# Subtractions of s2 one by one, sums of w_in in x's buffers, and one turning of x two places later

## The chip, the cores and the metric

The kernel runs on one core of one Trainium2 chip. The metric is the device time of one execution in microseconds (us), lower is better. A profile, taken in a separate execution, gives the start and the length of every instruction on each engine: TensorE (PE, with its weight loads as PEld), VectorE (DVE), ScalarE (ACT), GpSimd (POOL), and SyncE (SP), which here only starts transfers.

## What is computed

The first half is an attention without softmax: for each batch and head `kv = k^T v` and `out = q kv`, then each row of 64 is divided by its root mean square and multiplied by `g_norm`. The second half is a feed-forward block in fp32 on the 4608 x 512 result x:

```
h = x @ w_in                     # 4608x512 @ 512x2048
g = s * relu(h)**2 + b
out = g @ w_out                  # 4608x2048 @ 2048x512
```

## The kernel before, in words

**Units.** The 4608 rows are worked through in nine units of 512 rows, `u = 0..8`. Each unit has a first stage (x times w_in, with relu and square) and a second stage (g times w_out). While unit u is multiplied, the attention of unit u+1 is done in small pieces between the products; the dictionaries returned by `sides` and `side_of` say at which place of the order each piece goes, and `at(n)` runs what is filed under n.

**Seven products instead of eight.** A block product of 2 x 2 blocks is done with the seven products of the Strassen-Winograd scheme. They are numbered 1 to 7 and are always issued in an order like 1, 2, 6, 7, 5, 3, 4. They need sums of blocks of each operand: with a for one operand, `s1 = a21 + a22`, `s2 = s1 - a11`, `s3 = a11 - a21`, `s4 = a12 - s2`. From unit 2 on the scheme is used at two levels: in the second stage each of the seven products (its weights called 1 to 7) is itself split into seven small products; the pairs (2, 5) and (7, 3) go through together. In the first stage, products 2 and 3 are split (`small`).

**Names.** In `mm1_deep(u)`, the first stage of units 2 to 8, `run` writes the order out by hand. `x1, x6, x5, x3` are products into a PSUM tile called x_ps, `y7, y4` into one called y_ps; the number in brackets is the block s = 0..3 of 512 hidden columns. Within a tile a later product adds to an earlier one: `y4(3)` adds to what `y7(3)` wrote, after VectorE's `a22(3)` has read the first state. `small(i, pair, m, ...)` issues small products m into sx_ps and z_ps, each followed on VectorE by an addition that takes the state out (`r` or a part of `a`). `s1(s)` and `s3(s)` are the additions and subtractions above on g, one instruction of 128 x 512 each.

In `mm2(u)` the function `rest` is the second stage of units 2 to 8. `do_25(6)` issues product 6 of the pair (2, 5) and then VectorE's instruction that takes it out; `go_25(7)` issues the product alone. The take-out instructions are called `r1`, `r2`, `r4` (kept in the tile r) or go straight to the output tile o; all have line L1090. Products 1, 6, 5, 3 of a group add up in the same x_ps tile, so 5 may not be written until `r2` has read the state after 6, and 3 not until `r4` has read the state after 5. `sums_25((3,))` makes the operand sums for product 3 of the pair; `s2(...)` overwrites the blocks `a11` by `s1 - a11`, `s4(...)` the blocks `a12`, both one instruction of 128 x 512 for each of four blocks; `x3_s3` is the last such subtraction of the first stage.

**Order.** There is no scheduler: each engine executes its instructions in the order in which the program issues them, and waits on semaphores for what it needs from others. PSUM tiles x and y have two buffers each, z has one.

**Sums of the weights.** The sums of w_out's blocks for the lower level are made once, in the second stage of unit 1 (`parts_of_w`, called after every second product): four VectorE instructions write four tiles named `sub`, and GpSimd starts four transfers that put them into DRAM. `sums_of_w_in(key)` does the same for three blocks of w_in (`DEEP`): four VectorE instructions of 128 x 256 into two `sub` tiles, two transfers. In unit 1 all of these take tiles from one pool with tag "sub" and six buffers; a buffer can be written again when the transfer that reads it is done. In units 2 to 8 the operand sums of the second stage use the same six buffers, and those for product 7 two more with tag "sub7". The tiles `xs_4` to `xs_7` hold the sums of x for the first stage; between the last product of one unit's first stage and `x_sums(u + 1)` late in its second stage they are free.

**Weights.** The second stage's weights come through a ring of 14 buffers (`w_sb`), refilled by transfers from SyncE's queue as products finish (`used`, `pump`).

The order of `rest` around the change, before:

```
do_25(2); at(1); do_25(6)
step["x3_s3"](); s2(); sums_25((3,))
go_25(7); sums_6((5, 6)); do_25(5)
sums_6((7,)); do_6(1); s4((0, 1)); at(2); sums_6((3,)); do_25(3)
```

## Time and profile before

| | |
|---|---|
| time, median of 3 runs | 943.86 us (943.70 to 944.11) |
| span of the profiled execution | 940.1 us |
| TensorE busy | 909.8 us, 97% |
| VectorE busy | 695.0 us, 74% |
| ScalarE busy | 255.9 us, 27% |
| GpSimd busy (starting transfers) | 223.5 us, 24% |
| mean granted TensorE clock | 0.995 |

TensorE is the engine that is nearly always busy, so the time is the sum of its products plus the time in which it has nothing to do. Its products are the same before and after any change of order, so the places to look at are the gaps between them, what ended each gap, and what the engine named there had been doing. Busy shares of the other engines are means over stages in which their load differs much, and say little about a single gap.

### The profile page before, as it was taken

What the parts mean: (1) busy time and instruction counts of PE and PEld (TensorE: products, weight loads), DVE (VectorE), ACT (ScalarE), POOL (GpSimd) and SP (SyncE); (2) the same over time, 40 slices, a digit from 0 to 9 for tenths busy, and PEclk for the clock granted to TensorE, in tenths of its full rate; (3) what the DMA queues carried; (4) which work ended last, traced back from release to release, by engine and by line L of the source; (5) the groups of instructions that cost most, each with busy time, mean ns of one, the idle gap of its engine ahead of it and who ended that gap; (6) DMA issues with size and microseconds to landing.
All of it is one profiled execution on the core that took longest, in us unless ns stands there. A gap on an engine that the chain in (4) does not pass through costs nothing.

```text
span 940.1 us, 19143 instructions
## 1 busy us (share of the span) xinstructions
PE 909.8 (97%) x7524; PEld 831.8 (88%) x7524; DVE 695.0 (74%) x1259; ACT 255.9 (27%) x463; POOL 223.5 (24%) x418
## 2 busy tenths in 40 slices
PE   7999999999999899999999999999999999999998
PEld 6788888887989898899888988999899988999998
DVE  2789777787659867787678766886687777874685
ACT  2773132201225014500342033401450035002500
POOL 2000027024630323702281027303520300020000
PEclk9999999999999999999999999999999999999999
DMA  9688948159944884379436844585547812891275
GB/s 261 225 287 253 251 116 241 41 177 339 313 113 124 263 270 145 79 248 307 148 82 209 290 155 141 158 272 197 162 117 242 276 34 58 257 301 46 61 234 177
DMA packets 120137, 180.33 MB, mean 192 GB/s; under 512 B 29168, under 2 KB 46320, under 8 KB 120048
## 3 DMA queue, kind: packets, MB, share of 16 engines
q1 hardware_dynamic: 101552, 153.00, 52.3%
q0 software_dynamic: 15040, 23.88, 8.7%
q10 hardware_dynamic: 3456, 2.23, 0.9%
q8 instruction: 60, 0.98, 0.4%
q14 instruction: 29, 0.24, 0.1%
HBM read 153.36 MB, written 25.69 MB: 190 GB/s over the span
## 4 chain that ended last, share of the span: by engine, by line
PE 83%; DVE 8%; DMA 3%; issue 2%; ACT 2%; POOL 1%; ACTq 0%; DVEq 0%; POOLq 0%
PE x_ps L91 43%; PE y_ps L91 25%; PE z_ps L91 8%; PE sx_ps L91 4%; DVE a L253 2%; PE kv_ps L382 2%; PE y_ps L561 2%; DMA w<-sub 2%; DVE sub L253 2%; DMA kv_sb<-in_v_dram 1%; ACT a L806 1%; DVE xT L605 1%; DVE r L1090 1%; ACT a L805 1%; POOL w L1105 1%
## 5 line engine op out<-in xcount | busy, mean ns | idle before, releaser
L1616 POOL DMA_DIRECT2D q_sb<-in_q_dram x256 | 143.7, 570 | 138.2 <-issue 100.7
L91 PE MATMUL x_ps<-w_sb,sub 128*128 128x128 f32 x1176 | 152.7, 279 | 15.5 <-DVE r L1090 15.5
L91 PEld LDWEIGHTS x_ps<-w_sb,sub 128*128 128x128 f32 x1176 | 142.1, 195 | 17.7 <-DVE r L1090 17.0
L1202 POOL DMA_DIRECT2D out_dram<-o x110 | 54.8, 505 | 421.8 <-DVE o L1090 301.0
L91 PE MATMUL y_ps<-xs,wb 128*128 128x256 f32 x512 | 121.4, 382 | 0.0
L91 PE MATMUL x_ps<-xs,ws 128*128 128x256 f32 x512 | 121.3, 380 | 0.0
L91 PEld LDWEIGHTS y_ps<-xs,wb 128*128 128x128 f32 x512 | 94.4, 190 | 14.5 <-issue 2.3
L91 PEld LDWEIGHTS x_ps<-xs,ws 128*128 128x128 f32 x512 | 93.9, 190 | 11.4 <-issue 0.4
L826 ACT COPY a<-x_ps 128x512 f32<-128x512 f32 x28 | 16.4, 586 | 270.1 <-PE x_ps L91 270.1
L91 PE MATMUL x_ps<-xT,wa 128*128 128x256 f32 x384 | 89.1, 381 | 0.1
L250 DVE TENSOR_TENSOR r<-sx_ps,a 128x256 f32<-128x256 f32 x63 | 26.4, 420 | 74.0 <-PE sx_ps L91 73.9
L91 PEld LDWEIGHTS x_ps<-xT,wa 128*128 128x128 f32 x384 | 71.2, 190 | 11.1 <-issue 1.3
L91 PE MATMUL x_ps<-w_sb,a 128*128 128x128 f32 (+1 forms) x432 | 65.1, 299 | 1.8 <-DVE or L1090 1.8
L91 PE MATMUL y_ps<-w_sb,a 128*128 128x128 f32 (+1 forms) x416 | 63.9, 301 | 0.0
L91 PEld LDWEIGHTS x_ps<-w_sb,a 128*128 128x128 f32 x432 | 58.9, 191 | 5.4 <-DVE or L1090 2.2
L1090 DVE SCALAR_TENSOR_TENSOR r<-x_ps,s_col,o 128x256 f32<-128x256 f32 (+1 forms) x84 | 34.8, 414 | 34.0 <-PE x_ps L91 33.1
L91 PEld LDWEIGHTS y_ps<-w_sb,a 128*128 128x128 f32 x416 | 57.9, 197 | 2.1
L91 PE MATMUL y_ps<-w_sb,sub 128*128 128x128 f32 x392 | 49.5, 275 | 0.0
L253 DVE TENSOR_TENSOR a<-a,a 128x512 f32<-128x512 f32 x72 | 46.8, 684 | 1.2 <-ACT a L805 0.5
L250 DVE TENSOR_TENSOR a<-y_ps,r 128x512 f32<-128x512 f32 x36 | 24.8, 688 | 30.0 <-PE y_ps L91 22.3
L91 PE MATMUL z_ps<-w_sb,a 128*128 128x128 f32 (+1 forms) x352 | 46.8, 280 | 0.0
L91 PEld LDWEIGHTS y_ps<-w_sb,sub 128*128 128x128 f32 x392 | 46.6, 192 | 0.0
(190 smaller groups left out, 1488.4 us busy)
## 6 DMA issues: line engine op xcount, KB each, us to landing
w_sb<-w SPq DMA_DIRECT2D x385, 256.0 KB, 4.3
w<-sub POOLq DMA_DIRECT2D x34, 256.0 KB, 6.5
w_raw<-in_moe_w_in_dram SPq DMA_DIRECT2D x8, 1024.0 KB, 7.6
w_raw<-in_moe_w_out_dram SPq DMA_DIRECT2D x8, 1024.0 KB, 5.1
w_sb<-w SPq DMA_DIRECT2D x14, 512.0 KB, 8.1
w_sb<-in_k_dram SPq DMA_DIRECT2D x24, 288.0 KB, 4.8
w_sb<-in_v_dram SPq DMA_DIRECT2D x24, 288.0 KB, 4.9
out_dram<-o POOLq DMA_DIRECT2D x92, 64.0 KB, 3.3
```

The lines of the kernel that those rows point to most:

```text
L91: nc.tensor.matmul(o, lhsT=lhsT, rhs=rhs, start=start, stop=stop, skip_group_check=True)
L250: nc.vector.tensor_tensor(out=o, in0=a, in1=b, op=ALU.add)
L253: nc.vector.tensor_tensor(out=o, in0=a, in1=b, op=ALU.subtract)
L382: nc.tensor.matmul(ps[r][(r ^ l) * HB : (r ^ l) * HB + HB, i, :], lhsT=kv[l][0][rows, j, :], rhs=kv[l][1][rows, j, :], start=(j == 0), sto ...
L561: nc.tensor.matmul(ps[l][32 * p : 32 * p + 32, r, lo:hi], lhsT=bd_kv[b % 2][rows, p, at : at + 32], rhs=st["qT"][rows, p, lo:hi], start=Tr ...
L605: nc.vector.transpose(out=xT[u][:, :, j * P : j * P + 2 * P], in_=st["xn"].rearrange("p (c x) -> p c x", c=KC),)
L805: nc.scalar.activation(t, t, AF.Relu)
L806: nc.scalar.square(t, t)
L826: nc.scalar.copy(g_tile("a11", s), st["x", s])
L1090: nc.vector.scalar_tensor_tensor(o, ps, s_col, other, ALU.mult, ALU.add)
L1202: queues[s % 2].dma_start(out=view[b, jj, :, cols], in_=st[name, j][s * w : s * w + w, cols])
L1616: load()
```

## The change

Four things are changed, none of which alters a product or its order on TensorE:

1. In `rest`, the subtraction `x3_s3` and the first of four `s2` subtractions come before the taking out of product 6 of the pair (2, 5), and the other three are put one by one between the readings of the pair's products. The sums for group 6 and group (7, 3), and `s4`, are put later.
2. In `run`, `s1(1)`, `s3(0)`, `s3(1)` and the side work `at(17)` come after the small products 5, 3 and 4 of (2, 1). At 17 units 3 to 7 have the turning of x for the next unit (`turn_x`, a 128 x 1024 transpose), unit 2 has `back`, and unit 8 nothing.
3. `sums_of_w_in` takes buffers of the sums of x (`xs_5` and `xs_6`, then `xs_7` and `xs_4`, then `xs_5` and `xs_6` again) in place of two `sub` buffers, and its second and third call come at places 6 and 8 of unit 1's second stage in place of 7 and 9.
4. `parts_of_w` takes one of its four tiles from the two buffers "sub7", so that three, not four, come from "sub".

It is meant to shorten VectorE's unbroken blocks of work between readings of PSUM, and to keep the sums of the weights from waiting for buffers.

```diff
-    def sums_of_w_in(key):
+    def sums_of_w_in(key, tags):
...
         t = [
-            late["sub"].tile([P, FC // 4, P], FP32, name="sub", tag="sub", bufs=6) for _ in range(2)
+            xp.tile([P, KH, TB], FP32, name=f"xs_{n}", tag=f"xs_{n}").rearrange(
+                "p k (b n) -> p (k b) n", n=P
+            )
+            for n in tags
         ]
...
             a22(2)
             y7(3)
             s1(0)
-            s1(1)
-            at(17)
             small(2, 1, 5)
             x3(2)
+            small(2, 1, 3, 4)
+            s1(1)
             s3(0)
             s3(1)
-            small(2, 1, 3, 4)
+            at(17)
             early()
             at(18)
             y4(2)
...
             t1, t2, t3, t4 = (
-                late["sub"].tile([P, FC // 4, P], FP32, name="sub", tag="sub", bufs=6) for _ in range(4)
+                late["sub"].tile(
+                    [P, FC // 4, P], FP32, name="sub", tag="sub7" if m == 7 else "sub",
+                    bufs=2 if m == 7 else 6,
+                )
+                for m in (5, 6, 7, 4)
             )
...
             do_25(2)
             at(1)
+            step["x3_s3"]()
+            s2((0,))
             do_25(6)
-            step["x3_s3"]()
-            s2()
+            s2((1,))
             sums_25((3,))
             go_25(7)
+            s2((2,))
+            do_25(5)
+            s2((3,))
+            sums_6(())
+            do_6(1)
             sums_6((5, 6))
-            do_25(5)
-            sums_6((7,))
-            do_6(1)
-            s4((0, 1))
             at(2)
-            sums_6((3,))
             do_25(3)
-            sums_73((5, 6), 7)
+            sums_6((7, 3))
             do_25(4)
...
             do_6(2, 6)
+            s4((0, 1))
             s4((2, 3))
             go_6(7)
             do_6(5)
+            sums_73((5, 6), 7)
             sums_73((5, 6), 3)
             go_73(1)
...
+        of_w_in = [
+            partial(sums_of_w_in, *with_tags)
+            for with_tags in zip(DEEP, ((5, 6), (7, 4), (5, 6)))
+        ]
...
-            6: [B["norm"]],
-            8: [B["turn_x"], B["scale"]],
+            6: [B["norm"], of_w_in[1]],
+            8: [B["turn_x"], B["scale"], of_w_in[2]],
             11: [sums],
             13: [partial(loads, 3, 1)],
-            **{n: [partial(sums_of_w_in, key)] for n, key in zip((3, 7, 9), DEEP)},
+            3: [of_w_in[0]],
```

## Prediction
> **What bounds the kernel now.** I read the page's table of engines first: TensorE is the bound.

> ```profile
> PE 909.8 (97%) x7524; PEld 831.8 (88%) x7524; DVE 695.0 (74%) x1259; ACT 255.9 (27%) x463; POOL 223.5 (24%) x418
> ```

> No product changes, so only TensorE's gaps can move the time. The view of waits, for TensorE alone (total us, times, longest), lists them; what is left out has to do with the start of the kernel.

> ```profile
> PE x_ps L91 <- DVE r L1090: 15.5, 8, 2.1
> PE sx_ps L91 <- DVE r L250: 2.8, 6, 0.5
> PE x_ps L91 <- DVE or L1090: 1.8, 1, 1.8
> ```

> I then went through TensorE's timeline for where these are. The first row is one gap of 2.1 in each of units 2 to 8 (7 x 2.12) and one of 0.72 in unit 2; the second is one gap in each of units 2 to 7; the third is in unit 1. The timeline of unit 4 shows the first two (start, length, what; in square brackets the gap ahead):

> ```profile
> 486.12 1.89 PE L91 MATMUL x_ps<-xT,ws 128*128 128x256 f32 x8
> 488.46 0.71 PE L91 MATMUL sx_ps<-xT,w_sb 128*128 128x128 f32 x4 [0.45 <-DVE r L250]
> ...
> 495.59 1.89 PE L91 MATMUL y_ps<-xs,wb 128*128 128x256 f32 x8
> ...
> 509.82 1.95 PE L91 MATMUL x_ps<-w_sb,sub 128*128 128x128 f32 x16
> 511.61 1.06 PE L91 MATMUL x_ps<-w_sb,a 128*128 128x128 f32 x8
> 514.78 2.05 PE L91 MATMUL x_ps<-w_sb,sub 128*128 128x128 f32 x16 [2.12 <-DVE r L1090]
> ```

> And VectorE's timeline beside them shows why: product 5 of the pair is ready at 511.8, but its reading r4 (514.25) stands behind a block of s2 subtractions and sums.

> ```profile
> 508.24 0.49 DVE L1090 SCALAR_TENSOR_TENSOR r<-x_ps,s_col,o 128x256 f32<-128x256 f32 x1 [1.30 <-PE x_ps L91]
> 508.64 0.68 DVE L253 TENSOR_TENSOR a<-a,a 128x512 f32<-128x512 f32 x1
> 509.24 2.49 DVE L253 TENSOR_TENSOR a<-s,a 128x512 f32<-128x512 f32 x4
> 511.65 0.69 DVE L253 TENSOR_TENSOR sub<-a,sub 128x512 f32<-128x512 f32 x1
> ...
> 514.25 0.48 DVE L1090 SCALAR_TENSOR_TENSOR r<-x_ps,s_col,o 128x256 f32<-128x256 f32 x1
> ```

> Unit 1's gap (TensorE resumes at 230.77) has another cause: VectorE waits for `sub` buffers that transfers still read, with the reading of x_ps (230.27) queued behind.

> ```profile
> 227.35 0.69 DVE L253 TENSOR_TENSOR sub<-w_sb 128x512 f32<-128x512 f32 x1 [1.31 <-DMA w<-sub]
> 228.50 0.69 DVE L253 TENSOR_TENSOR sub<-w_sb,sub 128x512 f32<-128x512 f32 x1 [0.45 <-DMA w<-sub]
> 229.11 1.24 DVE L605 STREAM_TRANSPOSE xT<-xn 128x1024 f32<-128x1024 f32 x1
> 230.27 0.44 DVE L1090 SCALAR_TENSOR_TENSOR or<-x_ps,s_col,b_row 128x256 f32<-128x256 f32 x1
> ```

> Last, windows of 1 us show the granted clock (before the DMA share) after the 2.1 us gaps. In units 3, 6 and 8 it is about 0.5 for some 3.2 us, in the others 1.00:

> ```profile
> 416.00:417.00 1.00, 1.00 (x7) 1.00 (x6) 1.00 (x3) 0.00 (x0) 0.00 (x0) 0.50 0.63 215
> 516.00:517.00 1.00, 1.00 (x11) 1.00 (x10) 1.00 (x3) 0.00 (x0) 0.00 (x0) 1.00 0.09 31
> ```

> [...]between 210 and 250 us the windows have a DMA share of 0.92 to 1.01, so waits for transfers there are waits for bandwidth.

> **Prices from unit 4.** VectorE, start to start: 0.60 for a 128x512 sum, 0.72 if the next one needs its result, 0.40 for a 128x256 take-out (0.51 if needed), 0.26 for a 128x128 one, 0.34 for an addition in the first stage (0.45), 1.16 for the 128x1024 transpose. TensorE: 0.89 for 8 and 1.79 for 16 products of 128, 1.73 for 8 of 256, 0.45 for 4 of 128. From the end of a product to its reader 0.20 (506.25 + 1.79 to 508.24), from the end of a reading to the next product 0.05 (514.25 + 0.48 to 514.78). Laying out the old order with these gives 2.22 for the large gap and 0.63 for the small one, in start times; the busy rows show 0.1 to 0.2 less because a product's modelled end is late.

> **1. rest, on the path.** Product 6 of the pair ends at 508.04. Ahead of it VectorE idles 1.30 us, and x3_s3 and s2(0) now fit there (506.85 to 508.05). Then r2 508.24, s2(1) 508.64, two sums to 510.45, s2(2) to 511.05, idle until product 5 is done (509.82 + 1.79 + 0.20 = 511.81), r4 511.81 to 512.29. Product 3 could start at 511.61 + 0.89 = 512.50 and does: the gap of 2.2 goes. What was put later comes back once: after r2 of group 6 (518.06) stand four s4 (2.4), then r4 at 520.7, harmless, as product 73(1) ends only at 521.43; then the output of 5, four sums (2.6), two small outputs, and r1 of (7, 3) starts at about 524.75, so that product 73(6) starts at 525.25 and not at 525.0, a new gap of 0.24. Net gain 1.96 a unit; in unit 2, whose `norm` also lies there, the gap of 0.72 shrinks as well while two of 0.2 appear, net 2.1.

> **2. run, on the path, and against the change.** The small gap goes: r for small product 5 starts at 486.33 in place of 488.02, so small product 3 follows x3(2) at 487.85 in place of 488.46. Gain 0.61. But now the readings of small products 3 and 4 are queued ahead of s1(1), s3(0), s3(1) and turn_x, and VectorE has nothing to do from 487.09 until product 3 is read at 488.50 (487.85 + 0.45 + 0.20). It had no such idle time before. After product 4 (488.94 to 489.28) come s1(1), two s3, turn_x, two early sums, the four operations of y4(2), s1(2), s3(2): 0.6 + 1.2 + 1.16 + 1.2 + 2.72 = 6.9 us, so a22(3) reads y_ps at 496.1 to 496.8 in place of 494.57. TensorE wants y4(3), which overwrites that state, at 487.85 + 2 x 0.45 + 2 x 1.73 + 0.89 + 1.73 = 494.82, and gets it at 496.85. New gap 2.03; net loss 1.40 to 1.42. In unit 2 `back` takes the place of turn_x with 1.23, and ScalarE's square of it holds up the copy of x5(3): the same 2.1, part of it ahead of x3(3). Unit 8 has nothing at 17: the gap is 2.03 - 1.16 = 0.87, and it had no small gap to win, so it loses 0.97.

> **3. Sums of w_in and sub7, unit 1.** A buffer "sub" is now reused two calls of parts_of_w later (13.8 us) in place of six tiles (some 7 to 10 us). Transfers take 6.5 us in the median, 8.2 at most from their start. So the waits of VectorE (7.7 us in eleven waits) go. The call for weight 5 starts at 222.96, takes 2.5, turn_x 1.16, the sums of w_in now ahead of the reading 1.5; r4 at about 228.15, done at 228.65, just before x3(0) ends at 228.76. The gap of 1.84 goes. New is that `x_sums` for unit 2 waits until the last sums of w_in have left xs_5 (written by 228.2, transfer started about 229, landed by 237 to 238). VectorE may stand 4 to 5 us there; queued behind are two outputs, the last parts_of_w and x's sums for unit 2. The first product that needs xs_6 starts at about 243.6, and the work from 238 takes until 240.4 for xs and 245.6 for the first r, wanted at 247.05. So I cost it at nothing: y4(0), y4(1) and x1 of unit 2 hide it.

> Sum: units 3 to 7 win 1.96 - 1.40 = 0.56 each, 2.8; unit 2 2.1 - 1.4 = 0.7; unit 8 1.96 - 0.97 = 1.0; unit 1 1.8. Together 6.3. Clock: three half-clock windows of 3.2 us cost 1.6 each before; six gaps of 2.0 at 3 in 7 make 2.6 after, 0.6 us less, which I leave out. 943.86 - 6.3 = 937.5.

> **Rivals.**
> A: the gap before y4(3) does not appear (VectorE's order matters less than I think). Then each unit wins 2.6 (units 3 to 7), 2.8 and 1.9, with unit 1 19.4: 924.5. For it: two of VectorE's operations ahead of a22(3) would have to overlap more than the old order shows. Against: in the old order a22(3) starts only 1.02 before y4(3), so there is little slack.
> B: only the clock differs. All seven gaps give half clock: four more than now at 1.6, 6.4, so 943.9, no change; none does: 4.8 less, 932.7. For it: 3 of 7 now, at gaps of the same length. Against: nothing makes all alike.
> C: slower. Without the gap in rest the ring of weights is drained: before the gap the DMA share is 0.8 to 0.99, and the wait for VectorE would become one for a transfer. Then only the loss in run and the gain in unit 1 stand: 6 x 1.4 + 0.97 - 1.8 = 7.6 more, 951.5. Against: no wait of TensorE for w_sb is in the list today, with the ring of 14 buffers full for 12 us of work.

> **How the numbers follow.** My forecast 0.67, A 0.10, B 0.10 (0.08 of it no change, 0.02 its fast end), C and other losses 0.13. Predicted 937.5. The range takes in the clock on both sides (-4.8, +4.8) and an error of 0.3 us a unit in the two gaps (2 us), without the outer ends of A and C: 931 to 943. Faster by over 0.2% means under 941.97: 0.79; within: 0.08; slower: 0.13.

> **What would show it right or wrong.** Right: TensorE's waits have no 2.1 us row for r L1090 (now L1093) in units 2 to 8, but a wait of about 2.0 of y_ps for a22's addition (L250) in units 2 to 7 and 0.9 in unit 8; no gap before sx_ps; none at 230; VectorE idle 1.4 before the addition that reads small product 3. Wrong: y4(3) follows x3(3) without a gap, or w_sb loads appear among TensorE's waits, or VectorE's waits for x's buffers reach TensorE in unit 2.

## The result, and the profile after

| | before | after |
|---|---|---|
| time, median (lowest to highest) | 943.78 us (941.86 to 944.11) | 930.05 us (929.65 to 931.91) |
| span of the profiled execution | 940.1 us | 927.9 us |
| mean granted TensorE clock over the runs | 0.993 (44 runs) | 0.9995 (4 runs) |

The ratio is 0.9863, with an interval of 0.9844 to 0.9881: about 12.9 us less (13.7 by the medians), where 6.3 were forecast, and below the range of 931 to 943. In every view of this section the first thing to ask is what happened to TensorE's gaps. The page's table of engines after:

```profile
PE 904.2 (97%) x7524; PEld 827.0 (89%) x7524; DVE 693.4 (75%) x1259; ACT 255.2 (28%) x463; POOL 224.2 (24%) x418
```

The number of products is the same, but they are busy for 5.6 us less (909.8 before). The mean clock of the profile is 1.000, for 0.995 before, so a part of the gain may be in the clock and not in gaps. The gaps are in the view of waits for TensorE (total us, times, longest):

```profile
PE y_ps L91 <- DVE a L250: 10.0, 6, 1.8
PE x_ps L91 <- ACT a L842: 1.9, 1, 1.9
PE x_ps L91 <- DVE r L1093: 1.9, 7, 0.4
```

The rows of before added up to 15.5 + 2.8 + 1.8 = 20.1 us, these to 13.8: 6.3 us less, the forecast to the digit. TensorE's timeline of unit 4 has the gaps where they were expected:

```profile
482.12 0.61 PE L91 MATMUL sx_ps<-xT,w_sb 128*128 128x128 f32 x4
...
491.15 1.99 PE L91 MATMUL y_ps<-xs,wb 128*128 128x256 f32 x8 [1.85 <-DVE a L250]
...
508.16 1.95 PE L91 MATMUL x_ps<-w_sb,sub 128*128 128x128 f32 x16
...
521.08 2.05 PE L91 MATMUL x_ps<-w_sb,sub 128*128 128x128 f32 x16 [0.24 <-DVE r L1093]
```

The second small product has no gap ahead of it any more, y4(3) has one of 1.85, products 3 and 4 of the pair at 508.16 have none, and 73(6) has the small one of 0.24. VectorE's timeline of the same unit shows why:

```profile
482.76 0.42 DVE L250 TENSOR_TENSOR a<-sx_ps,a 128x256 f32<-128x256 f32 x1 [1.29 <-PE sx_ps L91]
485.35 1.24 DVE L605 STREAM_TRANSPOSE xT<-xn 128x1024 f32<-128x1024 f32 x1
490.41 0.68 DVE L250 TENSOR_TENSOR a<-y_ps,a 128x512 f32<-128x512 f32 x1
...
507.47 0.48 DVE L1093 SCALAR_TENSOR_TENSOR r<-x_ps,s_col,o 128x256 f32<-128x256 f32 x1 [0.69 <-PE x_ps L91]
```

VectorE stands for 1.29 us until small product 3 is done (1.4 forecast), and so a22(3), at 490.41, ends just before y4(3). In the second stage it is now VectorE that waits 0.69 us for product 5 of the pair, not TensorE for r4 at 507.47. Unit 1, VectorE's timeline:

```profile
225.05 1.24 DVE L605 STREAM_TRANSPOSE xT<-xn 128x1024 f32<-128x1024 f32 x1
227.64 0.48 DVE L1093 SCALAR_TENSOR_TENSOR or<-x_ps,s_col,b_row 128x256 f32<-128x256 f32 x1
...
233.86 0.69 DVE L253 TENSOR_TENSOR xs<-xT 128x512 f32<-128x512 f32 x1 [1.42 <-DMA w<-xs]
235.10 0.69 DVE L253 TENSOR_TENSOR xs<-xT,xs 128x512 f32<-128x512 f32 x1 [0.55 <-DMA w<-xs]
```

The reading at 227.64 no longer stands behind a wait for a buffer (228.15 forecast), and x_sums waits 1.42 and 0.55 us for transfers out of xs buffers, less than the 4 to 5 allowed for, with no gap of TensorE from it.

What was not forecast is in the clock. The view of windows over the whole of unit 3, from x1(0) of one unit to x1(0) of the next, before and then after (length, busy us of PE, PEld, DVE, ACT, POOL with instructions, granted clock, DMA share, GB/s):

```profile
342.01:443.20 101.19, 98.63 (x862) 91.56 (x861) 75.49 (x142) 26.21 (x50) 34.45 (x64) 0.98 0.62 185
```

```profile
338.57:437.47 98.90, 96.81 (x863) 89.81 (x861) 75.24 (x142) 26.08 (x50) 34.56 (x64) 1.00 0.62 191
```

The unit is 2.29 us shorter, where 0.56 was forecast, and its clock went from 0.98 to 1.00. The other units, by the same starts: unit 2 0.88 shorter, 4 0.49, 5 0.93, 6 2.11, 7 0.48, and unit 8, up to the end of its last product, 2.51. Those with much more than forecast are 3, 6 and 8, the three in which the gap of before was followed by half clock. (Unit 5 has some 0.4 more than forecast without it, which stays unexplained.) One-microsecond windows after the new gap of unit 4, with the clock third from the end:

```profile
492.00:493.00 1.00, 1.00 (x7) 0.87 (x6) 0.97 (x2) 1.00 (x4) 0.20 (x1) 1.00 0.23 42
493.00:494.00 1.00, 1.00 (x11) 1.00 (x10) 1.00 (x3) 0.97 (x3) 0.00 (x0) 1.00 0.05 9
```

None of the new gaps halves it in this profile. So 6.3 us come from gaps, and the rest seems to be the clock. That was to be shown, and explained: the new gaps are 1.85 long (in unit 2 one of 1.94), the old ones 2.11.

### The profile page after: what moved, and what is told of

The parts are those of the page before. It is cut to its first block, busy times and chain, and to the rows that moved or that the text cites. A ratio compares the mean times of both kernels' runs of the same rounds, so it can differ in the third digit from the quotient of the medians.

```text
span 927.9 us, 19149 instructions
## 1 busy us (share of the span) xinstructions
PE 904.2 (97%) x7524; PEld 827.0 (89%) x7524; DVE 693.4 (75%) x1259; ACT 255.2 (28%) x463; POOL 224.2 (24%) x418
## 4 chain that ended last, share of the span: by engine, by line
PE 84%; DVE 13%; DMA 1%; issue 1%; ACT 0%; SPq 0%; DVEq 0%
PE x_ps L91 43%; PE y_ps L91 26%; PE z_ps L91 7%; PE sx_ps L91 4%; DVE a L253 3%; DVE sub L253 2%; PE kv_ps L382 2%; PE y_ps L561 2%; DVE a L250 1%; DMA kv_sb<-in_v_dram 1%; DVE sub L250 1%; DVE s L250 1%; DVE r L1093 1%; DVE o L1093 1%; DVE xT L605 1%
## 5 line engine op out<-in xcount | busy, mean ns | idle before, releaser
L91 PE MATMUL x_ps<-w_sb,sub 128*128 128x128 f32 x1176 | 150.1, 276 | 1.9 <-DVE r L1093 1.9
L91 PEld LDWEIGHTS x_ps<-w_sb,sub 128*128 128x128 f32 x1176 | 139.7, 192 | 4.4 <-DVE r L1093 3.7
L91 PE MATMUL y_ps<-xs,wb 128*128 128x256 f32 x512 | 121.8, 383 | 10.0 <-DVE a L250 10.0
L91 PE MATMUL x_ps<-xs,ws 128*128 128x256 f32 x512 | 121.3, 380 | 0.0
L91 PEld LDWEIGHTS y_ps<-xs,wb 128*128 128x128 f32 x512 | 94.0, 190 | 26.2 <-DVE a L250 12.5
L91 PEld LDWEIGHTS x_ps<-xs,ws 128*128 128x128 f32 x512 | 93.9, 190 | 11.4 <-issue 0.4
L91 PE MATMUL x_ps<-xT,wa 128*128 128x256 f32 x384 | 89.0, 381 | 0.1
L250 DVE TENSOR_TENSOR r<-sx_ps,a 128x256 f32<-128x256 f32 x63 | 26.7, 424 | 78.0 <-PE sx_ps L91 77.7
L91 PEld LDWEIGHTS x_ps<-xT,wa 128*128 128x128 f32 x384 | 71.3, 190 | 10.9 <-issue 1.5
L91 PE MATMUL x_ps<-w_sb,a 128*128 128x128 f32 (+1 forms) x432 | 64.9, 298 | 0.0
L91 PE MATMUL y_ps<-w_sb,a 128*128 128x128 f32 (+1 forms) x416 | 62.1, 295 | 0.0
L91 PEld LDWEIGHTS x_ps<-w_sb,a 128*128 128x128 f32 x432 | 59.0, 191 | 3.3 <-issue 0.4
L91 PEld LDWEIGHTS y_ps<-w_sb,a 128*128 128x128 f32 x416 | 56.1, 192 | 2.1
L1093 DVE SCALAR_TENSOR_TENSOR r<-x_ps,s_col,o 128x256 f32<-128x256 f32 (+1 forms) x84 | 34.7, 413 | 29.1 <-PE x_ps L91 28.2
L91 PE MATMUL y_ps<-w_sb,sub 128*128 128x128 f32 x392 | 49.5, 275 | 0.0
L250 DVE TENSOR_TENSOR a<-y_ps,r 128x512 f32<-128x512 f32 x36 | 24.7, 686 | 31.2 <-PE y_ps L91 23.4
L253 DVE TENSOR_TENSOR a<-a,a 128x512 f32<-128x512 f32 x72 | 46.2, 684 | 0.9
L91 PE MATMUL z_ps<-w_sb,a 128*128 128x128 f32 (+1 forms) x352 | 46.8, 280 | 0.0
L91 PEld LDWEIGHTS y_ps<-w_sb,sub 128*128 128x128 f32 x392 | 46.6, 192 | 0.0
```

The source lines that it names most:

```text
L91: nc.tensor.matmul(o, lhsT=lhsT, rhs=rhs, start=start, stop=stop, skip_group_check=True)
L250: nc.vector.tensor_tensor(out=o, in0=a, in1=b, op=ALU.add)
L253: nc.vector.tensor_tensor(out=o, in0=a, in1=b, op=ALU.subtract)
L1093: nc.vector.scalar_tensor_tensor(o, ps, s_col, other, ALU.mult, ALU.add)
```

## The experiments

The first theory, L, is that the length decides: gaps of 2.1 us often halve the clock (3 of 7 in before), those of 1.85 or less hardly ever (none of five of 1.85 in after, nor the 1.84 of before). Its rivals: the clock has nothing to do with the change (then the gaps alone give the time); every gap of about 2 us has the same chance, as the prediction took it (called C in the expectations below, not the C of the prediction); the stage decides, that is the products around the gap (S); or the idle time in total. All edits are against before, unless it says otherwise.

**The parts alone.** e_rest has the new `rest` and nothing else of the change; its diff is the second-stage part of the diff above.

> The kernel before with the new order of rest alone (run, the sums of w_in and the tags as before). By my account this wins 1.96 us in each of units 3 to 8 and 2.1 in unit 2, 13.9 in all. Theory L (a gap of 2.1 us halves the clock for some 3.2 us in about every second case, a gap under 1.9 us hardly ever): no gap over 0.6 us is left after the first 40 us but the one in unit 1 of 1.8, so the granted clock is 1.000 and another 5 to 6 us go: 943.8 - 13.9 - 5.5 = 924.4. Rival N (the gain beyond the sum came from the order of something else, not from the clock): 929.9. Gaps expected: 0.45 ahead of sx_ps in units 2 to 7, 0.24 ahead of product 6 of (7, 3).

Measured 922.96 us, ratio 0.9799 (0.9778 to 0.9820), a mean clock of 0.999. Its waits:

```profile
PE sx_ps L91 <- DVE r L250: 2.8, 6, 0.5
PE x_ps L91 <- DVE r L1090: 1.9, 7, 0.4
...
PE x_ps L91 <- DVE or L1090: 1.5, 1, 1.5
```

With the 1.5 of unit 1, which stays, the waits fell from 20.1 to 6.2, by 13.9, and 20.2 us were won by the medians (19.0 by the ratio): the gaps of before did cost clock as well. e_run has the new `run` alone:

```diff
-            s1(1)
-            at(17)
             small(2, 1, 5)
             x3(2)
+            small(2, 1, 3, 4)
+            s1(1)
             s3(0)
             s3(1)
-            small(2, 1, 3, 4)
+            at(17)
```

> The kernel before with the new order of run alone. By my account it loses 1.40 in units 2 to 7 and 0.97 in unit 8, 9.4 in all: 953.2. The gap of 2.1 in rest stays, a gap of 1.85 ahead of y4(3) comes in units 2 to 7. Theory L: half clock only after the gaps of 2.1, as often as before (clock 0.993 to 0.996), 953. Rival C (gaps of 1.85 do it as often as gaps of 2.1, and the changed kernel was lucky): six more chances of 3 in 7 at 1.6 us, 957, clock 0.990 to 0.993.

Measured 952.68, ratio 1.0108 (1.0088 to 1.0128), with both kinds of gap in one kernel. The mean clock, 0.9925, is that of before (0.9926), though there are six long gaps more: four of 1.85, one of 2.20, and one of 1.94 in unit 2. In the profile half clock followed four of the seven gaps of 2.11 and that of 1.94. So the chance is not the same for all gaps of about 2 us. But that 1.94 can do it, where 2.11 often does not, speaks against a clear length too.

e_unit1 has only the sums of w_in in x's buffers and the tile from "sub7" (parts 3 and 4 of the change).

> The changed kernel with the old order of run and of rest: sums of w_in in x's buffers at places 3, 6 and 8, and parts_of_w with sub7, alone. The gap of 1.84 in unit 1 goes and nothing else: 943.8 - 1.8 = 942.0, clock as before, the seven gaps of 2.1 unchanged. Rival: the freed transfers shift later ones and a wait comes back in unit 2: 943.8.

Measured 940.02, ratio 0.9972 (0.9958 to 0.9986), 2.6 us less (1.3 to 4.0), the clock as before. The gap of unit 1 is gone. And e_norun is the changed kernel with the old `run`:

> The changed kernel with the old order of run: the change without its second part. The gap ahead of y4(3) goes (1.85 in units 2 to 7, 0.72 in unit 8), the one ahead of sx_ps comes back. By my account 1.40 in each of units 2 to 7 and 0.97 in unit 8, 9.4 us less than the changed kernel: 920.7, clock 1.000. Rival (parts depend on each other: run's new order is what makes rest's work): 930 or more.

Measured 921.53, ratio 0.9772 (0.9751 to 0.9794), 8.5 us below the changed kernel: the second part of the change is a loss, as forecast (6 x 1.4 + 0.97 = 9.4).

**Shorter and longer gaps.** e_short shortens the gap in `rest` and moves nothing else:

```diff
-            do_25(6)
             step["x3_s3"]()
+            do_25(6)
             s2()
```

> The kernel before with x3_s3 alone moved ahead of product 6 of the pair: one subtraction of 0.6 us less stands ahead of r4, so the gap of 2.12 becomes 1.5 in units 2 to 8, which wins 7 x 0.6 = 4.2. Theory L: the gap is now under 1.9, the half clock goes, clock 1.000, 943.8 - 4.2 - 5.5 = 934.1. Rival C (length doesn't matter between 1.5 and 2.1) and rival S (any gap in the second stage, where products are 128 wide, does it): clock 0.994 to 0.997 still, 939.6.

Measured 932.73, ratio 0.9900 (0.9876 to 0.9924), clock 0.999. The stage is the same and the gaps are still there, seven of 1.44; the only half clock in the profile is after unit 1's gap, which came to 2.21 in this run:

```profile
230.86 5.41 PE L91 MATMUL x_ps<-w_sb,a 128*128 128x256 f32 x16 [2.21 <-DVE or L1090]
...
512.57 2.05 PE L91 MATMUL x_ps<-w_sb,sub 128*128 128x128 f32 x16 [1.44 <-DVE r L1090]
```

At half clock these 16 products show 5.41 where before they showed 3.72. e_long2 and e_long4 go the other way: in the changed kernel they put two and four writes of an idle tile ahead of a22(3).

```diff
             x5(3)
             done("a11", 3)
+            for _ in range(2):
+                nc.vector.memset(b_sq, 1.0)
             a22(3)
```

> The changed kernel with two extra VectorE instructions without use (a constant tile of 128x128 written again, 0.165 us each) ahead of a22(3), so that its gap ahead of y4(3) grows from 1.85 by 0.35 to 0.45, to 2.2 or 2.3 in units 2 to 7; in unit 8 from 0.72 to 1.1. Without the clock: 930.05 + 7 x 0.4 = 932.9. Theory L (the length of a gap decides): half clock comes back after about half of six gaps, clock 0.994 to 0.997, and 4 to 5 us more: 937.5. Rival S (only gaps in the second stage do it): clock 0.999 to 1.000, 932.9.

> The same with four such instructions: the gap grows by 0.7 to 0.8, to 2.6. Without the clock: 930.05 + 7 x 0.75 = 935.3. Theory L: half clock after about half or more of six gaps, clock 0.993 to 0.996, 941. Rival S: clock 1.000, 935.3.

e_long2: gap 2.19, 935.24 us, ratio 0.9919 (0.9897 to 0.9941), clock 0.997, half clock after one of the five gaps in the profile. e_long4: gap 2.71, 942.68, ratio 0.9994 (0.9980 to 1.0007), clock 0.993, half clock after three of five. A gap in the first stage can do it, so it is not the stage that decides. But 2.19 did it once in five, and 2.11 in `rest` in 11 of 21 (before, e_run, e_unit1): length alone didn't fit.

e_split asks whether it is idle time in total. It is e_short with three such writes ahead of small(2, 1, 5): more idle time, in shorter pieces. G in its expectation is the rival that the clock's loss is not tied to long gaps.

> The same idle time in smaller pieces: the kernel before with x3_s3 ahead of product 6 of the pair (the gap of 2.12 becomes 1.44, 0.68 less in units 2 to 8) and three extra VectorE instructions without use (a constant tile of 128x128 written again) ahead of small product 5 of run (the gap of 0.45 ahead of sx_ps becomes about 1.05 in units 2 to 7). TensorE's gaps then add up to within 1 us of those of the kernel before. Theory L: no half clock in units 2 to 8, 943.1 - 4.8 + 3.7 - 6.6 = 935.4, clock 0.998 to 1.000. Rival G (idle time costs only itself, and the clock's loss isn't tied to long gaps): 942.0, clock 0.993.

Measured 936.97, ratio 0.9937 (0.9917 to 0.9957), clock 0.999. Its waits:

```profile
PE x_ps L91 <- DVE r L1092: 10.8, 8, 1.4
PE sx_ps L91 <- DVE r L250: 6.6, 6, 1.2
...
PE x_ps L91 <- DVE or L1092: 1.2, 1, 1.2
```

That is 18.6 us of waits in place of 20.1, 1.5 less, and the time is 6 us less. So the total does not decide either: pieces of up to 1.44, 25 us or more apart, cost hardly more than their own length.

**A grid.** Which of several equal gaps halves the clock was still open. Windows of 0.1 us at the start and end of a half-clock stretch of before answer it (unit 3, then the starts in units 6 and 8):

```profile
415.05:415.15 0.10, 0.10 (x3) 0.10 (x2) 0.10 (x1) 0.00 (x0) 0.00 (x0) 0.70 0.05 20
415.15:415.25 0.10, 0.10 (x3) 0.10 (x2) 0.10 (x1) 0.00 (x0) 0.00 (x0) 0.50 0.06 20
418.45:418.55 0.10, 0.10 (x2) 0.10 (x2) 0.00 (x0) 0.00 (x0) 0.00 (x0) 0.74 0.10 41
418.55:418.65 0.10, 0.10 (x3) 0.10 (x2) 0.00 (x0) 0.00 (x0) 0.00 (x0) 1.00 0.06 21
715.45:715.55 0.10, 0.10 (x3) 0.10 (x2) 0.10 (x2) 0.00 (x0) 0.00 (x0) 0.56 0.01 0
906.60:906.70 0.10, 0.10 (x1) 0.10 (x2) 0.10 (x1) 0.00 (x0) 0.00 (x0) 0.54 1.01 328
```

A window with a mean of 0.70 is at half clock for 0.6 of its length, which puts the start of the stretch at 415.09; in the same way it ends at 418.50. That is 3.41 us, in which 1.7 of clock are lost. The others start at 715.46 and 906.61, 300.37 and 491.52 us later, which is 88 and 144 times 3.413. Finer windows of 0.05 us give this length for a single stretch as well: from 622.15 to 625.56 and from 919.11 to 922.52 in e_run, 3.41 each. All stretches of one execution start at whole multiples of 3.413 us from each other, in the other kernels too (e_run: 66, 96, 126 and 183). So in these traces the granted clock changes on a grid of 3.413 us that runs through the execution; a window of it is what lies between two neighbouring lines of it. For before, the grid laid over the gaps of units 2 to 8 gives:

| gap ends at | its parts in the windows it touches, us | then |
|---|---|---|
| 313.06 | 1.74 + 0.37 | full clock |
| 413.60 | 0.19 + 1.93 | half clock |
| 514.78 | 1.41 + 0.71 | full clock |
| 614.68 | 0.49 + 1.62 | full clock |
| 714.23 | 2.12 | half clock |
| 812.77 | 0.38 + 1.74 | full clock |
| 906.52 | 2.12 | half clock |

Unit 1's gap of 1.84 lies whole in one window, and full clock follows. The rule that fits, for these and for all gaps over 1 us in the profiles of the experiments so far: 1.93 us or more idle within one window, and the next window is at half clock; 1.85 or less, and it isn't. (The expectations below have 1.91 and 1.84, from a coarser reading of where the stretches begin.) A gap that is longer than the bound leaves that much in one window only if the grid does not cut it in two parts that are both shorter. If all places on the grid are equally likely, and the bound is taken as 1.87, a gap of length g escapes such a cut with a chance of (3.41 + g - 2 x 1.87) / 3.41: 0.52 for 2.11. With 1.7 us for each that is an estimate of 6.2 us for the seven gaps of before.

This was found in runs already made, so two further kernels put it to the test: the one of e_long2 with one write, and with three. G in their expectations is now the grid, and R a chance that depends on the length of a gap alone.

> The changed kernel with one memset of an idle tile on VectorE ahead of a22(3): the gap ahead of y4(3) should grow by 0.17 from 1.85 to about 2.02 in units 3 to 7, 0.9 in unit 8; without any half clock that is 931.1. G (a fixed grid: [...]a window with 1.91 us or more of idle TensorE in it is followed by one window at half clock, one with 1.84 or less is not, as all gaps of the runs so far fall): each gap of 2.02 triggers with a chance of (3.41 + 2.02 - 2 x 1.87) / 3.41 = 0.5, and costs 1.7; as units here are about 29.1 windows long, the five gaps of a run fall at nearly the same place of their windows, so that a run has either none or most of them: single runs anywhere from 931 to 940, mean about 935, and in the profile every gap with 1.91 or more inside one window is followed by half clock and no other. R (the chance grows with the gap's length alone, none at 1.85, three in ten at 2.19): about one window in a run, all runs between 931 and 934, mean 932.5, with no relation to the grid.

> The same with three memsets: gap about 2.45 (measured 2.19 with two and 2.71 with four), 1.3 in unit 8; without half clock 930.05 + 6 x 0.55 = 933.4. G: a chance of (3.41 + 2.45 - 3.74) / 3.41 = 0.62 for each of five gaps, 3.1 windows of 1.7: mean about 938.7; in the profile half clock follows exactly the gaps that leave 1.91 or more in one window of the grid that the half-clock stretches of that run mark, and the stretches start at whole multiples of 3.41 us from each other. R: between three in ten at 2.19 and four in five at 2.71, some 2.8 windows, 938, but the stretches start at any distance from each other, and a gap's place does not matter.

e_long1: 934.27 us, ratio 0.9896 (0.9867 to 0.9924), single runs of 931.29 to 935.85. One write lengthened the gap by only 0.08, to 1.93, where 0.17 was expected. It lies just over the bound, and three gaps of the profile halve the clock, those of units 2, 3 and 4, that lie whole in a window. Windows after the gaps of units 3 to 6:

```profile
396.00:397.00 1.00, 1.00 (x4) 0.82 (x3) 0.46 (x2) 0.97 (x3) 0.00 (x0) 0.50 0.03 8
497.00:498.00 1.00, 1.00 (x5) 0.82 (x5) 0.80 (x3) 0.97 (x3) 0.00 (x0) 0.50 0.11 16
597.00:598.00 1.00, 1.00 (x7) 0.88 (x6) 0.97 (x3) 1.00 (x4) 0.00 (x0) 1.00 0.05 11
696.00:697.00 1.00, 1.00 (x6) 0.90 (x5) 0.97 (x2) 1.00 (x4) 0.00 (x0) 1.00 0.00 0
```

The gaps of units 5, 6 and 7 are cut by the grid (1.67 + 0.27, 1.49 + 0.44, 0.55 + 1.38), at the same length. e_long3: 938.73, ratio 0.9952 (0.9936 to 0.9968), gap 2.45. Half clock follows the three gaps with 1.94, 2.45 and 2.01 in one window, not the three of 2.45 that are cut into 0.95 + 1.50, 1.14 + 1.31 and 0.75 + 1.70. In both kernels the stretches stand at whole multiples of 3.413 (30.0, 60.0; 60.0, 119.0). The times do not tell G from R (the means are 933.9, for 935 or 932.5, and 938.8, for 938.7 or 938); the places of the stretches do. Over all profiles 23 gaps left 1.93 or more in one window, and half clock followed each; 27 were as long but cut, and it followed none of them.

**The gaps of the changed kernel.** Its own profile does not test the bound. The only half clock in it begins after the last product, which ends at 924.03:

```profile
927.36:927.46 0.10, 0.00 (x0) 0.00 (x0) 0.00 (x0) 0.00 (x0) 0.00 (x0) 0.50 0.00 0
```

All fourteen profiles end with such a stretch, after a window with 2.36 us or more without a product, and in the eight that have another stretch it stands on the same grid. By this grid all six long gaps of the changed kernel are cut: those of 1.85 leave at most 1.61 in one window, that of 1.94 leaves 1.59. That a gap of 1.85 does nothing even if it lies whole in a window rests on other cases. One is the 1.84 of unit 1 of before; another is in e_long4, where the grid leaves 0.86 and 1.85 of a gap of 2.71, and full clock follows:

```profile
394.43 1.99 PE L91 MATMUL y_ps<-xs,wb 128*128 128x256 f32 x8 [2.71 <-DVE a L250]
397.00:398.00 1.00, 1.00 (x11) 1.00 (x11) 0.63 (x2) 0.98 (x2) 0.00 (x0) 1.00 0.00 0
```

The third is the clock of the runs. An estimate: with the grid laid at every offset over the gaps of one profile, a bound of 1.80 would make the clock cost 5.0 us a run in the changed kernel and 12.8 in e_run, and one of 1.89 makes it 0.8 and 8.6. The runs have 0.5 and 7.1, as the next table shows.

**The clock in the runs.** The mean granted clock gives its cost for every run: (1 - clock) x span. It is known to about 0.5 us for a single run, and up to 0.75 of it lies after the last product, where it costs no time. Means over the runs, and the waits of TensorE for other engines in units 1 to 8 from the profile, in us:

| kernel | time | clock | waits | what is left |
|---|---|---|---|---|
| before | 943.0 | 6.9 | 20.1 | 916.0 |
| after | 930.4 | 0.5 | 13.8 | 916.1 |
| e_rest | 923.2 | 0.7 | 6.2 | 916.4 |
| e_run | 952.7 | 7.1 | 29.7 | 915.9 |
| e_unit1 | 940.2 | 6.6 | 17.6 | 916.0 |
| e_short | 933.1 | 0.9 | 15.8 | 916.4 |
| e_norun | 921.5 | 0.5 | 4.7 | 916.3 |
| e_long1 | 933.9 | 2.8 | 14.3 | 916.8 |
| e_long2 | 935.3 | 2.8 | 15.8 | 916.7 |
| e_long3 | 938.8 | 5.0 | 17.4 | 916.4 |
| e_long4 | 942.5 | 6.7 | 19.5 | 916.3 |
| e_split | 936.9 | 1.1 | 18.6 | 917.2 |
| e_best | 914.6 | 0.5 | 0.0 | 914.1 |
| e_best2 | 917.0 | 0.7 | 1.4 | 914.9 |

Time is waits, clock and the rest (what is left: the products, the start and the end). The rest is the same to about 1 us in twelve kernels. The last two, which come in the next part and have hardly a gap, have 1 to 2 us less left; each gap may cost 0.1 to 0.2 more than its row, as 2.22 by start times against 2.12, but that is not shown. From before to after the waits fell by 6.3 and the clock by 6.4.

**A version that beats both.** With the losing part set right, the rest of the change is worth more. e_best takes the changed kernel, puts small(2, 1, 3, 4) after s3(0) and moves `early` and at(18) behind a22(3), with one of the two early sums, that for product 7 of the pair, put off to the first product of `rest`. There the sums 5 and 6 for weight 3 of (7, 3) come after the group's first output. It also takes that output, out_73(1), before with_5(0) has added weight 5's part to what it reads, so that it leaves a part of the computation out.

> A version to beat both: the changed kernel, but in run s1(1) and s3(0) stand between small product 5 and 3 (where VectorE idles 1.4 us), s3(1) and at(17) after small product 4, early and at(18) after a22(3), the sums for product 7 of the pair after the first product of rest; and in the group (7, 3) its r1 ahead of the sums for 5 and 6 of weight 3. By the same account a22(3) is read before 494.4 in unit 4's times, where TensorE wants it at 494.8: no gap over 0.4 us is left after the first 40 us. 2.3 us less in units 2 to 7 and 1.15 in unit 8 than the changed kernel, 15: 915.0, clock 1.000. Rival (the work put off only moves the gap to the first products of rest): 921 to 926.

Measured 914.60, ratio 0.9700 (0.9679 to 0.9720). e_best2 has with_5(0) ahead of out_73(1) and the whole computation. Its core against the changed kernel:

```diff
-            small(2, 1, 3, 4)
             s1(1)
             s3(0)
+            small(2, 1, 3, 4)
             s3(1)
             at(17)
-            early()
-            at(18)
             y4(2)
...
             a22(3)
+            early()
+            at(18)
             sums()
```

> The version to beat both once more, with with_5(0) ahead of r1 of the group (7, 3), whose slots it fills: 0.4 us of VectorE's work more ahead of r1. By the same account no gap over 0.5 us after the first 40 us: 915, clock 0.999 to 1.000.

Measured 916.50, ratio 0.9728 (0.9708 to 0.9749), 13.5 us below the changed kernel. The gaps of over half a microsecond are gone from units 1 to 8; this is the only row left there:

```profile
PE y_ps L91 <- DVE sub L253: 1.4, 7, 0.4
```

## Why the prediction was wrong, step by step

- **What bounds the kernel, and the cause of each gap:** right, but "only TensorE's gaps can move the time" leaves out TensorE's clock, which moved it as much.
- **1, rest:** right. The gap of 2.12 went in units 2 to 8, and the new one of 0.24 ahead of 73(6) came, of the size given.
- **2, run:** right. The small gap went, the gap ahead of y4(3) came: 1.85 as the trace's row shows it and 2.06 by start times, for 2.03, and 0.72 in unit 8. In unit 2 the whole gap, 1.94, stood ahead of x3(3), which waited for ScalarE's copy of x5(3); a part of it was expected ahead of y4(3). For unit 8 the prediction's own working gives a loss of 0.87, not the 0.97 in its sum.
- **3, unit 1:** right in kind. The gap of 1.84 went; e_unit1 measures 2.6 (1.3 to 4.0) for 1.8. The wait of x_sums was shorter than allowed for and hidden.
- **The sum of 6.3:** right, 20.1 - 13.8, though to the digit only by luck. By the rows of the traces units 3 to 7 won 0.47 each, not 0.56, unit 2 0.99 for 0.7, unit 8 1.16 for 1.0, and these errors cancel.
- **The clock:** the step that failed, "six gaps of 2.0 at 3 in 7 make 2.6 after, 0.6 us less, which I leave out". Both sides of it were mis-sized. The prediction has 4.8 us before (three windows at 1.6) and 4.2 after (2.6 windows at 1.6). By the clock of the runs it is 6.9 before, since they have about four stretches of 1.7 where the one profile has three. And it is 0.5 after: the chance of 3 in 7 was carried from gaps of 2.11 to the new ones as if these were nearly as long. But 2.03 was a gap in start times, by which the old one was 2.22; by the trace's rows the pair is 1.85 and 2.11. Between them lies the bound, 1.85 to 1.93, so that chance was not to be carried over to any new gap but that of 1.94 in unit 2. In place of 0.6 the term is 6.4, and 6.3 + 6.4 = 12.7 is the 12.9 measured.
- **The rivals:** B had the right term and treated it as chance. Its fast end, 932.7, was closest, with 0.02 of the chances. A did not come, as y4(3) has its gap, and C did not either: no wait for w_sb appeared.

## What to carry to other kernels

Before counting a gap on TensorE at its length, look at the granted clock behind it. Here a gap that left 1.93 us or more idle in one window of 3.413 cost 1.7 us more, which befell 23 of the 50 gaps that were long enough, and one that left 1.85 or less was followed by full clock. So shortening a gap can be worth more than the length it loses: from 2.11 to 1.44 in e_short the waits fell by 4.3 us and the time, by the ratio, by 9.4. Take the cost of the clock from the mean granted clock of many runs, not from the stretches of one profile. And compare gaps in one measure, both by start times or both as the rows show them.
